# Engine orders from a list scheduler, bulk filter loads and DMA transposes in a one-core spectral and GLU kernel

## The chip, the core and the metric

The kernel runs on one core of a Trainium2 chip. The metric is device time in microseconds (us) of one execution. The engines are TensorE (PE; PEld are its weight loads), VectorE (DVE), ScalarE (ACT), GpSimd (POOL) and SyncE (SP), which issues most DMAs. Each engine runs its own list of instructions in order, and waits at an instruction until the semaphores that it names have been raised.

## What is computed

A layer norm of x, then two branches of the result that are added to x: a global filter (a two-dimensional real FFT, a product with complex weights, the inverse FFT) and a gated GELU feed-forward.

```python
x = A_x                                # 1 x 2048 x 512, bfloat16
xn = _layernorm(x, axis=-1)
# A: X = rfft2(xn) ; X = X * (w_r + 1j * w_i) ; y = irfft2(X)       w: 2048 x 257
# B: h = gelu(xn @ w_gate) * (xn @ w_up) ; y = h @ w_down           512 -> 1792 -> 512
return x + _A_ref(xn, A_w_r, A_w_i) + _B_ref(xn, B_w_gate, B_w_up, B_w_down)
```

## The kernel before

The 2048 rows of x are 16 "columns" c of 128 partitions (row 16p + c), kept in `x_t` and, normalised, in `xn`. Four columns are a block `sb` of 512 rows.

- **Loads.** SP and ACT issue x and the gate and up weights in slices, then the DFT tables (L179 to L191). The filter rows go to `TW`: 28 plain DMAs of 64 rows from SP (L206) and 18 indirect gathers of 128 rows from POOL (L208). `Wd_sb` is loaded whole behind them (L211).
- **`layernorm`** (L237): per column `bn_stats` and `bn_aggr` on DVE, the reciprocal root by ACT's Sqrt and a DVE reciprocal for the first four columns, by twelve small DVE steps (`rsqrt`, L221) for each later block, then `tensor_scalar` into `xn`.
- **`transposes`** (L254): eight PE transposes of 128x128 for two columns into PSUM (`tp`), and one DVE copy into `xnT`. All 16 columns go this way.
- **`glu`** (L412): for one of 14 slices `fc` of 128 hidden units, four matmuls with `Wg_sb` into `g_ps`, four with `Wu_sb` into `u_ps`, GELU on ACT into `ge`, the product on DVE into `hT`. Block 0 goes in halves of two columns (28 units of 256 columns), blocks 1 to 3 in units of 512 columns (42 units).
- **The filter branch.** `fold` (DVE) and `pstep` (64 PE matmuls `bp` of 128 columns, ACT copies into `Bs`) make the first DFT for a block; for each of eight groups g, `dstep` (`dp`, ACT copies `ds`), `cstep` (`ep`, ACT copies `E`), `filt` (some fifteen DVE operations with `TW`, then four DMAs F to F2 issued by SP, L364) and `icstep` (`gp`, ACT copies into `Gs`). `idstep` (`yp`) makes one column of the filter's output.
- **`down`** (L434): 14 matmuls with `Wd_sb` and one with `RI` into `y_ps`, the add of x on DVE (L443), the store (L444).

The order: the GLU units stand in a list (L449 to L455), the other steps are tasks with a due time counted in GLU time (L457 to L476), and the loop at L479 emits a task ahead of the unit at which it is due. The tile framework turns this program into each engine's list and places the waits. PSUM has four buffers with tag S and two each with G and U.

Of the kernel before, what the change touches and what calls it, by code (L numbers as in the profile page):

```python
# [28 lines left out]
def _tables():  # L29
# [80 lines left out]
    idx = np.zeros((P, NG, 2), dtype=np.int32)  # L110
    for g in range(NG):
        ks = 8 * g + 4 * h + a + 128 * kb
        if g == 0:
            ks = np.where((h == 0) & (a == 0) & (kb >= 8), 64 + 128 * (kb - 8), ks)
        idx[:, g, 0] = ks
        idx[:, g, 1] = (S - ks) % S
    idx[0, 0, 1] = S // 2
    return low(np.concatenate(parts, axis=1)), cols, low(RF), low(RI), idx.reshape(P, -1)
# [3 lines left out]
def kernel(  # L122
# [44 lines left out]
    def load_consts(first, last):
        a, b = ccols[first][0], sum(ccols[last])
        nc.sync.dma_start(out=CT[:, a:b], in_=cap[:, a:b])


    def load_x(c0, n, eng=nc.sync):
        eng.dma_start(out=x_t[:, c0:c0 + n, :], in_=x_v[:, c0:c0 + n, :])

    def load_w(a, b):
        nc.sync.dma_start(out=Wg_sb[:, :, a:b], in_=wg_v[:, :, a:b])
        nc.sync.dma_start(out=Wu_sb[:, :, a:b], in_=wu_v[:, :, a:b])

    load_x(0, 1)  # L179
    load_x(1, 1, nc.scalar)  # L180
    load_consts("ident", "ident")
    load_x(2, 2, nc.scalar)
    load_w(0, 256)
    load_w(256, 640)
    load_x(4, 4)
    load_w(640, 1216)
    load_x(8, 4)
    nc.sync.dma_start(out=RF_t[:], in_=rf_d.rearrange("p (c k) -> p c k", c=NC))
    load_w(1216, 1792)
    load_x(12, 4)  # L190
    load_consts("F0", "M0")  # L191

    W = 257
    idx_t = pc.tile([P, NG, 2], I32, name="idx_t")
    nc.gpsimd.dma_start(out=idx_t[:], in_=nc.inline_tensor(idx_np, name="spec_rows").ap()
                        .rearrange("p (g s) -> p g s", s=2))
    for T, w_in in ((TR, A_w_r), (TI, A_w_i)):  # L200
        rows = w_in.rearrange("(kb g h a) k -> h g kb a k", kb=NC, h=2, a=4)
        for g in range(NG):
            for s in range(2):
                if g > 0 and s == 0:
                    for h in range(2):
                        nc.sync.dma_start(out=T[64 * h:64 * h + 64, g, 0, 0:W], in_=rows[h, g])  # L206
                else:
                    nc.gpsimd.indirect_dma_start(  # L208
                        out=T[:, g, s, 0:W], out_offset=None, in_=w_in[:, :],
                        in_offset=bass.IndirectOffsetOnAxis(ap=idx_t[:, g, s:s + 1], axis=0))  # L210
    nc.sync.dma_start(out=Wd_sb[:], in_=wd_v)  # L211
# [4 lines left out]


    eps_t = pc.tile([P, 1], F32, name="eps_t")
    nc.vector.memset(eps_t[:], EPS)

    def rsqrt(y, var, n):  # L221

        V = nc.vector
        v = pw.tile([P, n], F32, name="v")
        t = pw.tile([P, n], F32, name="t")
        V.tensor_scalar(out=v[:], in0=var, scalar1=EPS, scalar2=None, op0=ALU.add)
        vi, ti, yi = v[:].bitcast(I32), t[:].bitcast(I32), y[:].bitcast(I32)
        V.tensor_scalar(out=ti, in0=vi, scalar1=1, scalar2=None, op0=ALU.logical_shift_right)
        V.tensor_scalar(out=yi, in0=ti, scalar1=-1, scalar2=0x5F3759DF, op0=ALU.mult, op1=ALU.add)
        for _ in range(3):  # L230
            V.tensor_tensor(out=t[:], in0=y[:], in1=y[:], op=ALU.mult)
            V.scalar_tensor_tensor(out=t[:], in0=v[:], scalar=-0.5, in1=t[:],
                                   op0=ALU.mult, op1=ALU.mult)
            V.scalar_tensor_tensor(out=y[:], in0=t[:], scalar=1.5, in1=y[:],
                                   op0=ALU.add, op1=ALU.mult)
# [18 lines left out]
    def transposes(c0):  # L254
        tp = ps.tile([P, NE, 2, P], BF16, name="tp", tag="S", bufs=4)
        for e in range(NE):
            for j in range(2):
                nc.tensor.transpose(tp[:, e, j, :], xn[:, c0 + j, e * P:(e + 1) * P], ident)  # L258
        nc.vector.tensor_copy(out=xnT[c0 // 4][:, :, c0 % 4:c0 % 4 + 2, :], in_=tp[:])


    fold_out = {}

    def fold(cg):
        V = nc.vector
# [3 lines left out]
        V.tensor_tensor(out=A[:, :, 0, :], in0=lo, in1=hi, op=ALU.add)
        V.tensor_tensor(out=A[:, :, 1, :], in0=lo, in1=hi, op=ALU.subtract)  # L270
        xf = pw.tile([P, 4, 4, P], BF16, name="xf")
        V.tensor_tensor(out=xf[:, :, 0:4:3, :], in0=A[:, :, :, 0:128], in1=A[:, :, :, 255:127:-1],
                        op=ALU.add)
        V.tensor_tensor(out=xf[:, :, 2:0:-1, :], in0=A[:, :, :, 0:128], in1=A[:, :, :, 255:127:-1],
                        op=ALU.subtract)
        fold_out[cg] = xf

    def pstep(cg, q):
        xf = fold_out[cg]
        bp = ps.tile([P, 4, P], F32, name="bp", tag="S", bufs=4)  # L280
        for j in range(4):
            nc.tensor.matmul(bp[:, j], lhsT=xf[:, j, q, :], rhs=RF_t[:, 4 * cg + j, :],  # L282
                             start=True, stop=True)
        o = Bs[:, q].rearrange("p g c r a -> p (c r) g a")[:, 8 * cg:8 * cg + 8]
        evac(o, bp[:].rearrange("p c (r g a) -> p (c r) g a", r=2, a=4))

    def evac(o, i):
        nc.scalar.copy(out=o, in_=i)  # L288
# [234 lines left out]
```

## Time and profile before

| | us |
|---|---|
| median of 3 timed runs | 198.29 (198.19 to 198.55) |
| the profiled execution, first to last instruction | 215.6 |
| PE busy in it | 184.0 |
| DVE busy | 126.2 |
| ACT busy | 90.3 |
| POOL busy | 20.3 |

The profiled execution is one run of its own, taken with the profiler on, and is 17.3 us longer than the median; the page gives no other time for it than the span. Busy time of PE counts each matmul up to its modelled end, so that neighbours overlap; the pace is read from the chain, where a group of matmuls follows another without a gap. A line such as "x4" counts the instructions in a group. [...]

### The profile page before, as it was taken

What the parts mean: (1) busy time and instruction counts of PE and PEld (TensorE: products, weight loads), DVE (VectorE), ACT (ScalarE), POOL (GpSimd) and SP (SyncE); (2) the same over time, 40 slices, a digit from 0 to 9 for tenths busy, and PEclk for the clock granted to TensorE, in tenths of its full rate; (3) what the DMA queues carried; (4) which work ended last, traced back from release to release, by engine and by line L of the source; (5) the groups of instructions that cost most, each with busy time, mean ns of one, the idle gap of its engine ahead of it and who ended that gap; (6) DMA issues with size and microseconds to landing.
All of it is one profiled execution on the core that took longest, in us unless ns stands there. A gap on an engine that the chain in (4) does not pass through costs nothing.

```text
span 215.6 us, 3193 instructions
## 1 busy us (share of the span) xinstructions
PE 184.0 (85%) x1136; PEld 102.2 (47%) x1136; DVE 126.2 (59%) x316; ACT 90.3 (42%) x170; POOL 20.3 (9%) x33
## 2 busy tenths in 40 slices
PE   0581009999889999999999899999999999999993
PEld 0451006787665545455445445444454444545441
DVE  3970006999998339978578487493353544255421
ACT  2310002353618566787778768754341212121100
POOL 1777740100000000000000000000000000000000
PEclk9998555999999999999999999999999999999999
DMA  5999732760000200101202202202002222222211
GB/s 166 362 382 380 205 76 49 223 213 3 0 2 3 97 0 2 41 19 40 49 0 52 50 0 55 49 0 49 0 3 73 73 73 85 70 91 72 77 49 49
DMA packets 17503, 17.69 MB, mean 82 GB/s; under 512 B 2208, under 2 KB 16304, under 8 KB 17488
## 3 DMA queue, kind: packets, MB, share of 16 engines
q1 hardware_dynamic: 16592, 15.90, 24.1%
q0 software_dynamic: 608, 1.19, 1.9%
q10 hardware_dynamic: 288, 0.39, 0.6%
q8 instruction: 9, 0.15, 0.3%
q14 instruction: 6, 0.05, 0.1%
HBM read 13.29 MB, written 2.10 MB: 71 GB/s over the span
## 4 chain that ended last, share of the span: by engine, by line
PE 57%; DVE 17%; another core or an unknown queue 7%; issue 6%; DMA 5%; ACT 5%; SPq 2%; DVEq 0%
PE y_ps L438 22%; PE u_ps L428 12%; PE g_ps L425 12%; ACT E L310 3%; DVE stats L242 2%; SPq L364 2%; PE tp L258 2%; DVE hT_187 L432 2%; PE dp L295 2%; PE yp L393 2%; PE y_ps L440 2%; DMA x_t<-in_A_x_dram 1%; PE bp L282 1%; DVE hT_1164 L432 1%
## 5 line engine op out<-in xcount | busy, mean ns | idle before, releaser
L431 ACT ACTIVATE ge<-g_ps 128x512 bf16<-128x512 f32 (+1 forms) x70 | 35.4, 517 | 52.2 <-PE g_ps L425 26.3
L428 PEld LDWEIGHTS <-Wu_sb 128*128 128x128 bf16 x280 | 28.3, 101 | 35.2 <-issue 14.9
L425 PEld LDWEIGHTS <-Wg_sb 128*128 128x128 bf16 x280 | 28.6, 104 | 23.2 <-issue 5.2
L443 DVE TENSOR_TENSOR y_sb<-y_ps,y_sb 128x512 bf16<-128x512 f32 x16 | 11.1, 692 | 30.2 <-PE y_ps L440 30.2
L425 PE MATMUL g_ps<-xnT_70,Wg_sb 128*128 128x256 bf16 x112 | 19.4, 300 | 10.5 <-issue 10.5
L428 PE MATMUL u_ps<-xnT_70,Wu_sb 128*128 128x256 bf16 x112 | 18.5, 297 | 7.8 <-DVE hT_187 L432 7.0
L399 ACT CAST yf<-yp 128x512 bf16<-128x512 f32 x16 | 9.2, 587 | 37.3 <-PE yp L393 37.3
L432 DVE TENSOR_TENSOR hT_187<-u_ps,ge 128x256 bf16<-128x256 f32 x28 | 11.6, 419 | 19.6 <-remote 16.0
L310 ACT CAST E<-ep 64x512 bf16<-64x512 f32 x32 | 18.5, 579 | 4.0 <-PE ep L307 3.7
L425 PE MATMUL g_ps<-xnT_72,Wg_sb 128*128 128x512 bf16 x56 | 15.4, 384 | 0.0
L425 PE MATMUL g_ps<-xnT_71,Wg_sb 128*128 128x512 bf16 x56 | 15.0, 381 | 0.0
L425 PE MATMUL g_ps<-xnT_73,Wg_sb 128*128 128x512 bf16 x56 | 14.9, 380 | 0.0
L428 PE MATMUL u_ps<-xnT_72,Wu_sb 128*128 128x512 bf16 x56 | 14.9, 379 | 0.0
L428 PE MATMUL u_ps<-xnT_73,Wu_sb 128*128 128x512 bf16 x56 | 14.9, 379 | 0.0
L428 PE MATMUL u_ps<-xnT_71,Wu_sb 128*128 128x512 bf16 x56 | 14.4, 380 | 0.0
L432 DVE TENSOR_TENSOR hT_807<-u_ps,ge 128x512 bf16<-128x512 f32 x14 | 9.6, 687 | 7.0 <-PE u_ps L428 6.7
L258 PE MATMUL tp<-CT,xn 128*128 128x128 bf16 x64 | 6.5, 243 | 7.7 <-DVE xn L250 7.6
L438 PE MATMUL y_ps<-Wd_sb,hT_187 128*128 128x512 bf16 x56 | 12.7, 379 | 0.0
L438 PE MATMUL y_ps<-Wd_sb,hT_807 128*128 128x512 bf16 x56 | 12.7, 379 | 0.0
L438 PE MATMUL y_ps<-Wd_sb,hT_1164 128*128 128x512 bf16 x56 | 12.7, 379 | 0.0
L242 DVE BATCH_NORM_STATS2 stats<-x_t 128x6 f32<-128x512 bf16 x16 | 10.6, 678 | 3.4 <-DMA x_t<-in_A_x_dram 3.4
L288 ACT CAST Bs<-bp 128x512 bf16<-128x512 f32 x16 | 8.5, 598 | 6.3 <-PE bp L282 6.3
(126 smaller groups left out, 242.0 us busy)
## 6 DMA issues: line engine op xcount, KB each, us to landing
y_sb<-in_A_x_dram SPq DMA_DIRECT2D x16, 128.0 KB
out_dram<-y_sb SPq DMA_DIRECT2D x16, 128.0 KB
Wd_sb<-in_B_w_down_dram SPq DMA_DIRECT2D x1, 1792.0 KB
x_t<-in_A_x_dram SPq DMA_DIRECT2D x3, 512.0 KB
Wg_sb<-in_B_w_gate_dram SPq DMA_DIRECT2D x2, 576.0 KB
Wu_sb<-in_B_w_up_dram SPq DMA_DIRECT2D x2, 576.0 KB
RF_t<-spec_rf SPq DMA_DIRECT2D x1, 512.0 KB
RI_t<-spec_ri SPq DMA_DIRECT2D x1, 512.0 KB
```

Source lines behind the costliest of these rows:

```text
L242: nc.vector.bn_stats(out=stats[:, j, :], in_=x_t[:, c0 + j, :])
L258: nc.tensor.transpose(tp[:, e, j, :], xn[:, c0 + j, e * P:(e + 1) * P], ident)
L288: nc.scalar.copy(out=o, in_=i)
L295: nc.tensor.matmul(dp[:, q % 2, :, q // 2], lhsT=Bs[:, q, G].rearrange("p c r a -> p (c r a)"), rhs=FQ[q], start=(q == 0), stop=(q == 3), ...
L310: nc.scalar.copy(out=E[64 * h:64 * h + 64, r], in_=ep[64 * r:64 * r + 64])
L399: nc.scalar.copy(out=yf[:, c % 2], in_=yp[:])
L425: nc.tensor.matmul(gp[:], lhsT=Wg_sb[:, e, fc * P:(fc + 1) * P], rhs=rhs[:, e, :], start=(e == 0), stop=(e == NE - 1))
L428: nc.tensor.matmul(up[:], lhsT=Wu_sb[:, e, fc * P:(fc + 1) * P], rhs=rhs[:, e, :], start=(e == 0), stop=(e == NE - 1))
L431: nc.scalar.activation(out=ge[:], in_=gp[:], func=AF.Gelu_apprx_tanh)
L432: nc.vector.tensor_tensor(out=hT[sb, fc][:, o:o + w], in0=up[:], in1=ge[:], op=ALU.mult)
L438: nc.tensor.matmul(y_ps[:], lhsT=hT[sb, f][:, cl * P:(cl + 1) * P], rhs=Wd_sb[:, f, :], start=(f == 0), stop=False)
L443: nc.vector.tensor_tensor(out=y_sb[:], in0=y_ps[:], in1=y_sb[:], op=ALU.add)
```

## The change

Every operation becomes an entry of a plan (`_Plan`): engine, duration in us, what it depends on, a priority, the buffers that it takes and uses. `run` steps through time and gives each engine, whenever it is free, the entry with the lowest priority number whose inputs are there by the durations written in it. The order found is emitted as it is, under `tc.manual_schedule()`. Beside that:

- columns 0 and 1 are normalised and transposed alone, then 2 and 3; block 0's GLU runs `fc` 0 and 1 in units of one, one and two columns, `fc` 2 to 13 in units of 512 columns;
- from column 4 on, `xnT` is written by DMA transposes issued by SP, one of 128 x 512 for each column;
- the reciprocal root is two POOL operations (`tensor_scalar`, then `tensor_tensor` with `pow`) on all columns of a step;
- filter rows: four plain loads of 64 partitions x 7 rows and two gathers of 128 x 7 rows go to `Ts`, which shares its buffer with `Wd`; twelve ACT copies (`spread`) bring them to `TW`; four gathers of one row each remain; the frequency order in the tables `RF` and `RI` is changed to suit;
- `Wd` is loaded in two halves once the spreads are done;
- nine matmuls of 512 columns on a memset tile `warm` go first on PE;
- the last column's `down`, add and store go in two halves.

```diff
+class _Plan:
+    HOP = 0.1
...
+                best = None
+                for o in ops:
+                    if any(d.end is None for d in o.deps):
+                        continue
+                    at = max([d.end + d.lag + self.HOP for d in o.deps if d.eng != "PE" or o.eng != "PE"] + [0.0])
...
+                    if best is None or (o.prio, o.n) < (best.prio, best.n):
+                        best = o
...
+    def spread(k, s, g0, g1):
+        T = (TR, TI)[k]
+        src = tiles["Ts"][:, k, s].rearrange("p (g k) -> p g k", k=KC)
+        src = src[:, g0 - 1:g1 - 1] if s == 0 else src[:, 7 - g1 + 1:7 - g0 + 1][:, ::-1]
+        nc.scalar.copy(out=T[:, g0:g1, s, 0:KC], in_=src)
...
+    NWARM = 9
+    def warm_mm(i):
+        if i == 0:
+            psum("warm", [P, D])
+        nc.tensor.matmul(tiles["warm"][:], lhsT=warm[:, 0:P], rhs=warm[:], start=True, stop=True)
...
+        e = add("POOL", 0.25, lambda: nc.gpsimd.tensor_scalar(
+            out=ve[:, k], in0=mv[:, k, 1], scalar1=1.0, scalar2=EPS, op0=ALU.mult, op1=ALU.add), ag, due - 5, lag=0.1)
+        r = add("POOL", 0.3, lambda: nc.gpsimd.tensor_tensor(
+            out=rstd[:, k], in0=ve[:, k], in1=half[:, k], op=ALU.pow), (e, o_mem[1]), due - 5, lag=0.1)
...
+    def dma_transpose(c, due):
+        XT[c] = dma(P * D * 2, lambda: nc.sync.dma_start_transpose(out=xnT[c // 4][:, :, c % 4], in_=xn[:, c]),
+                    (XN[c],), due - 30, lag=1.0)
...
+    for c0, n, due in ((0, 1, -20), (1, 1, -19), (2, 2, -18)):
+        layernorm(c0, n, due)
+        for c in range(c0, c0 + n):
+            pe_transpose(c, due)
+    for b, due in ((1, 16), (2, 24), (3, 32)):
+        layernorm(4 * b, 4, due)
+        for c in range(4 * b, 4 * b + 4):
+            dma_transpose(c, due)
...
+    units = [(0, 1, 0), (0, 1, 1), (1, 1, 0), (1, 1, 1), (2, 2, 0), (2, 2, 1)]
+    units += [(0, 4, fc) for fc in range(2, NFC)]
...
+    T_FOLD, D_FOLD = 22.0, 5.0
+    T_D, D_D = 44.0, 6.5
...
+                ex.append(dma(64 * 1024, mv_, [last] + ex[:1], t, new=(f2,) if not ex else (), use=(fb, f2), lag=0.5,
+                              issue=0.1))
...
+        parts = 2 if c == NC - 1 else 1
...
+    order = plan.run()
+    with tc.manual_schedule():
+        for o in order:
+            o.fn()
```

## Rows read from the trace of the kernel before

**Rows 1.** The page, section 1: busy us, share of the span, instructions.
```profile
PE 184.0 (85%) x1136; PEld 102.2 (47%) x1136; DVE 126.2 (59%) x316; ACT 90.3 (42%) x170; POOL 20.3 (9%) x33
```

**Rows 2.** Busy time by stretch; columns in the first line.
```profile
core 0: us, PE busy (x) PEld busy (x) DVE busy (x) ACT busy (x) POOL busy (x), PEclk, DMA share, GB/s
7.15:16.13 8.98, 7.69 (x48) 5.53 (x49) 7.17 (x18) 1.84 (x3) 6.84 (x8) 1.00 1.07 378
16.13:32.64 16.51, 1.38 (x6) 0.65 (x5) 0.56 (x3) 1.15 (x3) 10.61 (x16) 0.62 0.69 218
32.64:37.12 4.48, 4.48 (x22) 3.09 (x22) 2.77 (x10) 0.77 (x2) 0.00 (x0) 0.50 0.21 49
42.00:60.00 18.00, 16.16 (x168) 13.16 (x166) 17.84 (x58) 8.57 (x21) 0.27 (x2) 1.00 0.26 88
60.00:75.00 15.00, 14.36 (x112) 8.71 (x112) 10.71 (x29) 8.12 (x16) 0.00 (x0) 1.00 0.11 37
75.00:157.00 82.00, 79.85 (x445) 40.10 (x444) 55.38 (x125) 56.56 (x101) 0.00 (x0) 1.00 0.12 27
157.00:212.10 55.10, 55.10 (x302) 26.63 (x299) 23.21 (x48) 9.17 (x16) 0.00 (x0) 1.00 0.21 68
```

**Rows 3.** Waits: who waited for whom, us in total, times, longest us.
```profile
ACT ge L431 <- remote: 18.2, 3, 6.9
DVE hT_187 L432 <- remote: 16.0, 1, 16.0
```

**Rows 4.** The chain that ended last: start us, us, what.
```profile
0.74 2.97 DMA x_t<-in_A_x_dram
...
9.85 1.01 PE g_ps L425 x4
...
43.26 0.49 PE tp L258 x8
...
44.89 0.44 PE u_ps L428 x4
...
69.01 0.45 PE bp L282 x8
...
74.86 0.44 PE dp L295 x4
...
157.52 3.02 PE y_ps L438 x14
...
212.26 0.69 DVE y_sb L443
```

**Rows 5.** Groups by line and form: count, busy us, mean ns, idle before.
```profile
L432 DVE TENSOR_TENSOR hT_187<-u_ps,ge 128x256 bf16<-128x256 f32 x28 | 11.6, 419 | 19.6 <-remote 16.0 <-PE u_ps L428 1.7 <-issue 1.2
L242 DVE BATCH_NORM_STATS2 stats<-x_t 128x6 f32<-128x512 bf16 x16 | 10.6, 678 | 3.4 <-DMA x_t<-in_A_x_dram 3.4
L288 ACT CAST ds<-dp 128x512 bf16<-128x512 f32 x16 | 9.0, 596 | 3.1 <-PE dp L295 3.1
L208 POOL DMA_INDIRECT TW<-in_A_w_r_dram,idx_t x9 | 8.8, 981 | 6.2 <-DMA idx_t<-spec_rows 3.8 <-issue 2.4
L250 DVE TENSOR_SCALAR xn<-x_t,mv,rstd 128x512 bf16<-128x512 bf16 x16 | 5.8, 423 | 0.1
L243 DVE BATCH_NORM_AGGREGATE mv<-stats 128x2 f32<-128x6 f32 x16 | 2.6, 172 | 0.0
L234 DVE SCALAR_TENSOR_TENSOR rstd<-t,rstd 128x4 f32<-128x4 f32 x9 | 1.4, 157 | 0.1
L259 DVE COPY xnT_72<-tp 128x1024 bf16<-128x1024 bf16 x2 | 1.3, 691 | 0.0
L325 POOL TENSOR_SCALAR TW<-tt 128x8 bf16<-128x8 f32 x4 | 0.9, 258 | 0.0
```

**Rows 6.** The F exchange of one group: SP's issues, and the chain's piece.
```profile
95.68 2.38 SPq L364 DMA_DIRECT2D F_1064<-F  x4
...
97.47 2.00 DMA F_1064<-F
```

More of the change, by code (lines that the diff above doesn't have):

```diff
@@ L109, in _tables @@
     h, kb, a = np.arange(P) // 64, np.arange(P) // 4 % 16, np.arange(P) % 4
[L110 to L118, printed above, removed]
+    ks = 128 * kb + 32 * h + 8 * a
@@ L158, with cc @@
     RF_t = pc.tile([P, NC, P], BF16, name="RF_t", tag="RF")
-    late = {}
     TW = pc.tile([P, 2, NG, 2, 258], BF16, name="TW", tag="TW")
     TR, TI = TW[:, 0], TW[:, 1]
-    def cc(name, shape=None):
+    idx_t = pc.tile([P, 3], I32, name="idx_t")
+    mv = pc.tile([P, NC, nc.vector.BN_AGGR_DIM], F32, name="mv")
+    ve = pc.tile([P, NC], F32, name="ve")
+    rstd = pc.tile([P, NC], F32, name="rstd")
+    half = pc.tile([P, NC], F32, name="half")
+    warm = pc.tile([P, D], BF16, name="warm")
+    tiles = {}
+    def cc(name):
         o, w = ccols[name]
         return CT[:, o:o + w]
[L167 to L211, printed above, removed]
     ident = cc("ident")
@@ L215 @@
     IQ = [cc(f"I{q}") for q in range(4)]
[L218 to L235, printed above, removed]
@@ L254, in transposes @@
[L254 to L265, printed above, removed]
+    plan = _Plan({"S": 4, "G": 2, "U": 2, "ge": 3, "A": 1, "xf": 2, "ds": 4, "E": 2, "X": 2,
+                  "Y": 2, "F": 2, "F2": 2, "y": 3})
@@ new lines, with dve, act, pe @@
+    add = plan.op
+    PSUM_LAG = 0.2
+    OVER = {"PE": 0.0, "DVE": 0.08, "ACT": 0.08, "POOL": 0.1}
+    def dve(n, fn, deps, prio, **k):
+        return add("DVE", n, fn, deps, prio, lag=0.08, **k)
+    def act(n, fn, deps, prio, **k):
+        return add("ACT", n, fn, deps, prio, lag=0.08, **k)
+    def pe(n, fn, deps, prio, **k):
+        return add("PE", n, fn, deps, prio, lag=PSUM_LAG, **k)
+    def dma(nbytes, fn, deps, prio, eng="SP", issue=0.5, **k):
+        return add(eng, issue, fn, deps, prio, nbytes=nbytes, **k)
@@ new lines, in load_ct @@
+    def load_ct(first, last, eng="SP"):
+        a, b = ccols[first][0], sum(ccols[last])
+        q = nc.sync if eng == "SP" else nc.scalar
+        return load(P * 2 * (b - a), lambda: q.dma_start(out=CT[:, a:b], in_=cap[:, a:b]), eng=eng)
+    load_x(0, 1)
+    load_x(1, 1, "ACT")
+    d_ident = load_ct("ident", "ident", "ACT")
+    load_w(0, 2, ("SP", "ACT"))
+    load_x(2, 2)
+    load_w(2, 4)
+    load_x(4, 4)
+    load_w(4, 7)
+    load_x(8, 4)
+    load_w(7, 10)
+    load_w(10, 14)
+    load_x(12, 4)
@@ new lines, with load_wd @@
+    for k in range(2):
+        for s in range(2):
+            for g0, g1 in ((1, 3), (3, 5), (5, 8)):
+                d_tw.append(act(0.2 + (g1 - g0) * 0.215, lambda k=k, s=s, g0=g0, g1=g1: spread(k, s, g0, g1),
+                                d_st[k, s], 40 + len(d_tw)))
+    def load_wd(k):
+        if "Wd" not in tiles:
+            tiles["Wd"] = pc.tile([P, NFC, D], BF16, name="Wd_sb", tag="Wd")
+        nc.sync.dma_start(out=tiles["Wd"][:, 7 * k:7 * k + 7], in_=wd_v[:, 7 * k:7 * k + 7])
@@ new lines @@
+    d_wd = [load(P * 7 * D * 2, lambda k=k: load_wd(k), d_tw[:12]) for k in range(2)]
+    for T, w_in in ((TR, A_w_r), (TI, A_w_i)):
+        for s in range(2):
+            d_tw.append(add("POOL", 1.2, lambda T=T, w_in=w_in, s=s: nc.gpsimd.indirect_dma_start(
+                out=T[:, 0, s, 0:KC], out_offset=None, in_=w_in[:, :],
+                in_offset=bass.IndirectOffsetOnAxis(ap=idx_t[:, s:s + 1], axis=0)), (g_idx, XD[12]), 20, lag=4.0))
+    o_mem = [add("POOL", 0.3, lambda: nc.gpsimd.memset(warm[:], 1.0), (), -20, lag=0.05),
+             add("POOL", 0.2, lambda: nc.gpsimd.memset(half[:], -0.5), (), -15, lag=0.05)]
@@ L269, in fold @@
[L269 to L288, printed above, removed]
@@ new lines, with dstep, mm, ev @@
+    d_fix = add("POOL", 3.0, tables_fix, d_tw, 60, lag=0.2)
+    def dstep(G, t):
+        sb, db = _Buf("S"), _Buf("ds")
+        def mm():
+            dp = psum(f"dp.{G}", [P, 2, P, 2])
+            for q in range(4):
+                nc.tensor.matmul(dp[:, q % 2, :, q // 2], lhsT=Bs[:, q, G].rearrange("p c r a -> p (c r a)"),
+                                 rhs=FQ[q], start=(q == 0), stop=(q == 3), skip_group_check=True)
+        def ev():
+            ds = work(f"ds.{G}", [P, D], "ds")
+            nc.scalar.copy(out=ds[:], in_=tiles[f"dp.{G}"][:].rearrange("p s k t -> p (s k t)"))
+        p = pe(0.34, mm, [PS_[cg, q] for cg in range(4) for q in range(4)] + [d_ct], t, new=(sb,))
+        DS_[G] = act(0.53, ev, (p,), t - 5, new=(db,), use=(sb,)), db
@@ L434, in down @@
-    def down(c):
-        sb, cl = c // 4, c % 4
-        y_ps = ps.tile([P, D], F32, name="y_ps", tag="S", bufs=4)
-        for f in range(NFC):
-            nc.tensor.matmul(y_ps[:], lhsT=hT[sb, f][:, cl * P:(cl + 1) * P], rhs=Wd_sb[:, f, :],
-                             start=(f == 0), stop=False)
-        nc.tensor.matmul(y_ps[:], lhsT=late["RI"][:, c, :], rhs=late["yt"][:, c, :], start=False, stop=True)
-        y_sb = pw.tile([P, D], BF16, name="y_sb", bufs=3)
-        nc.sync.dma_start(out=y_sb[:], in_=x_v[:, c, :])
-        nc.vector.tensor_tensor(out=y_sb[:], in0=y_ps[:], in1=y_sb[:], op=ALU.add)
-        nc.sync.dma_start(out=out_v[:, c, :], in_=y_sb[:])
@@ L477, with mv_ @@
[L477 to L492 removed]
+                def mv_(h=h, r=r):
+                    if h == 0 and r == 0:
+                        work(f"F2.{g}", [P, 2, 2, 256], "F2")
+                    nc.sync.dma_start(out=tiles[f"F2.{g}"][64 * r:64 * r + 64, h],
+                                      in_=tiles[f"F.{g}"][64 * h:64 * h + 64, r])
@@ new lines, with load_ri @@
+    for g in range(NG):
+        t = T_D + D_D * g
+        dstep(2 * g, t)
+        dstep(2 * g + 1, t)
+        cstep(g, t + 2)
+        filt(g, t + 3)
+        icstep(g, t + 8)
+    for sb in range(1, NSB):
+        for fc in range(NFC):
+            extra = [o for cg in range(4) for o in FOLD[cg]] + [XT[c] for c in range(4, NC)] if sb == 2 else ()
+            glu(4 * sb, 4, fc, extra)
+    ID_ = {}
+    T_END = now[0]
+    all_ic = [o for g in range(NG) for o in IC_[g]]
+    d_ri = []
+    def load_ri():
+        tiles["RI"] = pc.tile([P, NC, P], BF16, name="RI_t", tag="RF")
+        nc.sync.dma_start(out=tiles["RI"][:], in_=ri_d.rearrange("p (c k) -> p c k", c=NC))
```

591 lines of the change are left out of this document (418 added, 173 removed).

## Prediction

> **What bounds the kernel now.** I read the page's first lines, then busy time by stretch, then the waits, then the chain of work that ended last, then the groups of instructions. Section 1 of the page says that PE is busy for 184.0 of 215.6 us [rows 1], so the question is what PE's time is made of. The chain gives its real pace: fourteen matmuls of 512 columns in `down` take 3.02 us (0.216 each, and the GLU's of 512 have the same shape), four of 256 columns 0.44 us (0.110 each), eight transposes 0.49 us (0.061 each), eight `bp` 0.45 us (0.056 each), four `dp` 0.44 us (0.109 each) [rows 4]. Counted by the loops in the code: 336 x 0.216 = 72.5 and 224 x 0.110 = 24.6 for the GLU, 240 x 0.216 = 51.8 for `down`, 64 x 0.061 = 3.9 for the transposes, 192 x 0.056 = 10.8 for `bp`, `gp` and `yp` (taken as equal, all 128 columns), 64 x 0.109 = 7.0 for `dp`, 16 x 0.216 = 3.5 for `ep`. That is **174.1 us of work at full pace**; the other 41.5 us of the span are lost to waits and to the lower clock.
>
> Where they are lost: 7.15 us pass before PE's first transpose, since the stretches begin there [rows 2]. From 7.15 to 16.13 PE ran 48 matmuls (16 transposes and 32 of 256 columns, 4.5 us of work in 8.98), so 4.5 are lost. From 16.13 to 32.64 it ran 6 in 16.51 us [rows 2]: 15.9 lost. [...] The last matmul is followed by the add at 212.26 [rows 4] and the store: 3.4 lost to the end of the span. 8.5 are left for 37 to 212. PE stands idle for 2.48 us in 42 to 75, for 2.15 in 75 to 157 and for none in 157 to 212 [rows 2]; in that proportion the 8.5 are about **4.5 in 37 to 75 and 4.0 in 75 to 157**. In 42 to 60 DVE is busy for 17.84 of 18 us: that stretch is bound by DVE. `down` runs without a gap.
>
> **The stop from 16.13 to 32.64 I take out of the sum.** ACT and DVE waited there 18.2 and 16.0 us for a release that the trace can place on no engine [rows 3]. The median of the timed runs is 198.29, 17.3 us under this span, and the stop with the slow clock behind it is 15.9 + 2.1 = 18.0. 215.6 - 18.0 = 197.6, so the timed runs can't contain it; the 0.7 between 197.6 and the median stays as it is on both sides.
>
> **The change, part by part.** (1) *Transposes.* 48 of the 64 leave PE: 48 x 0.061 = **2.9 off the work**; they ran between GLU matmuls, on the path. 12 DMA transposes of 128 KB take their place on SP's queue, behind all bulk loads. (2) *GLU shape.* 28 units of 256 columns become 12 of 512, two of 256 and four of 128: 24.6 becomes 96 x 0.216 + 16 x 0.110 + 32 x 0.056 = 24.3, **0.3 off**. Work after: 174.1 - 3.2 = 170.9.
>
> (3) *Start.* Before, the first GLU matmul is at 9.85 behind two-column steps [rows 4]. After, the first column goes alone: its load lands at 3.71, statistics 0.68, aggregate 0.17, two small POOL operations, normalise 0.42 [rows 4, 5], four transposes and a copy of half size. POOL's `pow` is in no row: its nearest row is 0.258 for a small POOL operation, with a hop 0.35; bounded by 0.2 below and by the 0.98 of POOL's DMA issue above I take 0.7 for the pair (0.5 to 2). At half clock a 256-column matmul takes 0.25 [rows 4], so four transposes take about 0.5, and the copy 0.4. First GLU matmul at 7.0. Columns 2 and 3 need two statistics more on DVE, POOL and two copies, and come to PE at about 10.5; by then PE has done 16 transposes and four small units, 2.8 at full pace, and small units at half pace (3.6) just fill 7.0 to 10.6. So about 7.7 are lost up to 10.5, and up to 1.2 more if the clock is still low until 13. I take **8.5 (7.5 to 10)** for the 7.15 + 4.5 = 11.65 of before.
>
> (4) *The clock.* [...] After, nine matmuls on a memset tile run from about 1.3 to 5.1 us, where PE stood idle; nothing waits for them, and their cost is nothing unless they delay the first transpose at about 5.8. [...]
>
> (5) *DVE's stage.* Off DVE in the stretch that it bounds: six copies of transposes x 0.691 = 4.1; 36 Newton steps x 0.157 = 5.6 (to two POOL operations a block); 28 products x 0.419 = 11.7 become about 10.2. Sum 11.2 of DVE's 28.6 busy us in 42 to 75 [rows 2, 5]. PE's 4.5 lost there become **1.2 (0.3 to 3)**; late next is ACT, which gets 12 spread copies. Their nearest row is 0.596 for 512 elements; at 514 and 771 elements they are 8 x 0.6 + 4 x 0.9 = 8.4 us. ACT is idle for 16 of the 33 us of 42 to 75 [rows 2], which hides them; without that cover a GELU is late by up to 0.9 each.
>
> (6) *Filter rows.* 28 SP issues and 18 gathers become 4 and 8. PE does not wait for them before or after, since the first product with them comes after `ep`: nothing. They free SP's queue, where the DMA transposes go, and 10 gathers x 0.98 on POOL, so that `pow` is not queued behind these. The second half of the loads now waits for `Wd`'s buffer to come free after the spreads, 100 us ahead of `down`: nothing.
>
> (7) *Order.* From 75 to 157 PE waits for the F exchange: four issues on SP take 2.38 us and the last lands 2.00 us after its issue [rows 6], some 3.9 in all. The plan puts `icstep` behind two modelled landings in a row, so later than 3.9. But it lets the spectral groups come closer (a group to 6.5 us, PE's own 1.75 in it): ACT's eight copies x 0.596 and 2.8 GELUs make 6.4 of that. I take **3.0 (1.5 to 5)** for 4.0. (8) *End.* The last column in halves: **3.0 (2.7 to 3.4)** for 3.4.
>
> Sum: 170.9 + 8.5 + 1.2 + 3.0 + 3.0 = 186.6, and with the 0.7 **187.3**. Best ends: 170.9 + 7.5 + 0.3 + 1.5 + 2.7 + 0.7 = 183.6. Worst: 170.9 + 10 + 3 + 5 + 3.4 + 0.7 = 193.0.
>
> **Rivals.** *A, the DMA transposes make PE wait, and the kernel gets slower.* No row shows a DMA transpose. PE reaches block 1 at about 10.5 + 2 x 0.9 + 12 x 1.73 + 1.8 (`bp`) = 35; its four columns are normalised at about 17. At t us each, one after the other, they are there at 17 + 4t. Nearest rows: a plain 128 KB load took 2.97 [rows 4], a 64 KB exchange within the chip 2.00 [rows 6]; at 3 they are there at 29 and cost nothing. At t = 7 PE waits 10 us for block 1 and 1 us more for each of the blocks 2 and 3, which are 27 us of PE apart: 12, and all is given back. From there the kernel is slower: at 8 us each 14 + 5 + 5 = 24, that is 211. For it: SP issues in order, and a queue of waiting transposes holds the F exchange too. Against: twice the nearest rows.
>
> [...]
>
> *C, the change does not do what it says.* The order written down is about the one that ran, and only the transposes, shape, start and end count: 197.6 - 2.9 - 0.3 - 3.2 - 0.4 + 0.7 = 191.5. For: before, too, each engine ran a list fixed in advance. Against: DVE's removed work is off whatever the order. *D, better.* DVE's stage and the middle lose nearly nothing and the clock is up at 10.5: 182 to 183.5.
>
> **How the numbers follow.** The forecast (183.5 to 190) 0.60, B 0.17, C 0.07, D 0.06, A 0.10. Faster by over 0.2% (what a measurement here can tell) is all but A: 0.89, with 0.01 within and 0.10 slower. The range runs from D's edge to the worst ends, 183.0 to 193.5, and leaves out A, most of D and a little of B.
>
> **What would show it.** First GLU matmul near 7.0 instead of 9.85; 16 `tp` matmuls left; no stretch with DVE full while PE waits for a product; no wait of PE for `xnT` with a DMA as releaser; the F exchange no longer a releaser of `gp`; `down` without gaps at 0.216. A stop like the one at 16 us may show or not, and says nothing of timed runs. The forecast is wrong if PE waits for `xnT`, if `pow` shows at over 1 us, or if ACT has no idle time between 40 and 100 us.

## The result and the profile after

| | before | after |
|---|---|---|
| median of the timed runs, us | 198.24 (198.06 to 198.55, 4 runs) | 188.24 (188.04 to 189.37, 4 runs) |
| the profiled execution, us | 215.6 | 186.3 |

The ratio is 0.951, with an interval of 0.948 to 0.954: 10.0 us off. The profiled execution of the changed kernel is itself one of the timed runs, 188.04 us at a span of 186.3, so 1.7 us of a time lie outside its span. The median is 0.9 above the forecast of 187.3 and well inside the range. The span was forecast at 186.6 and is 186.3: of the 0.9, 1.0 is the term for what lies outside the span (0.7 for 1.7), 0.2 is that this run is the fastest of the four, and the span takes 0.3 back.

Section 1 of the page of the changed kernel (engine, busy us, share of the span, instructions; some matmul records are missing from this trace), to be read beside [rows 1]:

```profile
PE 176.2 (95%) x1014; PEld 93.5 (50%) x1032; DVE 119.2 (64%) x264; ACT 93.2 (50%) x169; POOL 16.7 (9%) x35
```

Its busy time by stretch, to be read beside [rows 2] (PEclk is the granted share of TensorE's full clock):

```profile
core 0: us, PE busy (x) PEld busy (x) DVE busy (x) ACT busy (x) POOL busy (x), PEclk, DMA share, GB/s
7.78:9.09 1.31, 1.01 (x8) 0.84 (x9) 1.31 (x5) 0.00 (x0) 0.00 (x0) 0.53 1.03 370
9.09:13.85 4.76, 3.59 (x41) 3.24 (x40) 3.39 (x13) 1.11 (x4) 0.89 (x2) 0.77 1.07 352
13.85:40.00 26.15, 25.99 (x150) 13.65 (x154) 25.01 (x59) 15.95 (x30) 11.61 (x16) 1.00 1.09 250
40.00:75.00 35.00, 34.79 (x206) 19.02 (x208) 26.66 (x56) 29.22 (x53) 1.21 (x6) 1.00 0.31 89
75.00:127.00 52.00, 51.69 (x302) 27.47 (x307) 36.85 (x81) 37.39 (x67) 0.00 (x0) 1.00 0.16 35
127.00:131.30 4.30, 3.80 (x36) 2.42 (x35) 4.19 (x12) 3.83 (x8) 0.00 (x0) 1.00 0.00 0
131.30:183.10 51.80, 51.59 (x273) 25.64 (x275) 18.85 (x38) 4.42 (x8) 0.00 (x0) 1.00 0.23 72
```

From 13.85 us to the end of the matmuls PE stands idle for about 1.4 us in all: 0.16 + 0.21 up to 75, 0.31 + 0.50 up to 131.3, 0.21 in `down`. There is no stop. What is left to lose is ahead of 13.85. PE's list there (start, us, operation, count, and in brackets the idle time before it with its releaser):

```profile
1.31 3.64 PE L409 MATMUL warm<-warm 128*128 128x512 bf16 x9 [1.31 <-POOL half L402]
7.78 1.01 PE L444 MATMUL tp<-CT,xn 128*128 128x128 bf16 x8 [2.83 <-DVE xn L434]
9.09 0.59 PE L496 MATMUL g_ps<-xnT,Wg_sb 128*128 128x128 bf16 x4 [0.30 <-DVE xnT L447]
11.89 0.90 PE L444 MATMUL tp<-CT,xn 128*128 128x128 bf16 x8
13.85 0.61 PE L496 MATMUL g_ps<-xnT,Wg_sb 128*128 128x256 bf16 x4 [1.05 <-DVE xnT L447]
```

The first GLU matmul is at 9.09, not at 7.0, and columns 2 and 3 reach it at 13.85, not at 10.5. 16 transposes and 32 matmuls of 128 columns are 2.8 us of work, so 13.85 - 2.8 = 11.05 are lost. DVE's list says why (same columns):

```profile
4.00 1.29 DVE L421 BATCH_NORM_STATS2 st<-x_t 128x6 f32<-128x512 bf16 x2 [4.00 <-DMA x_t<-in_A_x_dram]
6.71 0.69 DVE L421 BATCH_NORM_STATS2 st<-x_t 128x6 f32<-128x512 bf16 x1 [1.21 <-DMA x_t<-in_A_x_dram]
7.33 0.72 DVE L434 TENSOR_SCALAR xn<-x_t,mv,rstd 128x512 bf16<-128x512 bf16 x2
11.06 0.29 DVE L510 TENSOR_TENSOR hT<-u_ps,ge 128x128 bf16<-128x128 f32 x1 [0.56 <-PE u_ps L496]
11.27 0.40 DVE L434 TENSOR_SCALAR xn<-x_t,mv,rstd 128x512 bf16<-128x512 bf16 x1
```

POOL has the roots of columns 0 and 1 from 6.01 to 7.11, but in the fixed order the statistics of column 2 stand ahead of `xn` of column 0, and wait until 6.71 for a load. Columns 2 and 3 have their roots at 10.52, and their `xn` stands behind a product that waits until 11.06 for matmuls, at a granted clock of 0.50 from 8.00 to 11.26.

The groups of the two POOL operations by form (busy us, mean ns of one), and the DMA transposes: SP's list (start, us of issuing) and the page's line (median us from issue to landing):

```profile
L431 POOL TENSOR_TENSOR rstd<-ve,half 128x4 f32<-128x4 f32 x3 | 3.1, 1020 | 0.2
L431 POOL TENSOR_TENSOR rstd<-ve,half 128x1 f32<-128x1 f32 x2 | 1.1, 564 | 0.1
L429 POOL TENSOR_SCALAR ve<-mv 128x1 f32<-128x1 f32 x2 | 0.4, 192 | 3.5 <-DVE mv L428 3.4
```

```profile
19.63 13.73 SPq L451 DMA_TRANSPOSE xnT<-xn  x8
xnT<-xn SPq DMA_TRANSPOSE x12, 6.3
```

No wait of PE names a transpose as its releaser.

### The profile page after: what moved, and what is told of

Same layout as the page of the kernel before. It is cut to its first block, busy times and chain, and to the rows that moved or that the text cites. A ratio compares the mean times of both kernels' runs of the same rounds, so it can differ in the third digit from the quotient of the medians.

```text
span 186.3 us, 2911 instructions
## 1 busy us (share of the span) xinstructions
PE 176.2 (95%) x1014; PEld 93.5 (50%) x1032; DVE 119.2 (64%) x264; ACT 93.2 (50%) x169; POOL 16.7 (9%) x35
## 4 chain that ended last, share of the span: by engine, by line
PE 90%; DMA 3%; DVE 2%; ACT 2%; issue 1%; SPq 0%; DVEq 0%
PE g_ps L496 26%; PE u_ps L496 26%; PE dp L600 4%; DMA x_t<-in_A_x_dram 3%; PE bp L564 2%; PE gp L737 2%; PE ep L619 2%; PE yp__1693 L837 2%; PE yp__2023 L837 2%; PE yp__1880 L837 2%; PE yp__1849 L837 2%; PE yp__1804 L837 2%; PE yp__1784 L837 2%; PE yp__1744 L837 2%; PE yp__1725 L837 2%; PE yp__2049 L837 2%
## 5 line engine op out<-in xcount | busy, mean ns | idle before, releaser
L496 PE MATMUL g_ps<-xnT,Wg_sb 128*128 128x512 bf16 (+2 forms) x232 | 58.4, 370 | 1.7 <-DVE xnT L447 1.4
L496 PE MATMUL u_ps<-xnT,Wu_sb 128*128 128x512 bf16 (+2 forms) x235 | 58.3, 368 | 0.3
L510 DVE TENSOR_TENSOR hT<-u_ps,ge 128x512 bf16<-128x512 f32 (+2 forms) x60 | 39.0, 651 | 23.5 <-PE u_ps L496 21.7
L505 ACT ACTIVATE ge<-g_ps 128x512 bf16<-128x512 f32 (+2 forms) x60 | 34.2, 570 | 32.0 <-PE g_ps L496 29.2
L837 PEld LDWEIGHTS <-hT 128*128 128x128 bf16 x238 | 23.0, 98 | 23.6 <-issue 0.2
L421 DVE BATCH_NORM_STATS2 st<-x_t 128x6 f32<-128x512 bf16 x16 | 10.4, 668 | 5.2 <-DMA x_t<-in_A_x_dram 5.2
L605 ACT CAST ds<-dp 128x512 bf16<-128x512 f32 x16 | 8.6, 592 | 2.6 <-PE dp L600 2.6
L743 ACT CAST Gs<-gp 128x512 bf16<-128x512 f32 x16 | 8.7, 589 | 0.8 <-PE gp L737 0.8
L600 PE MATMUL dp<-CT,Bs 128*128 128x128 bf16 x64 | 8.3, 309 | 0.0
L660 DVE TENSOR_TENSOR m<-X,TW 128x1024 bf16<-128x1024 bf16 x8 | 5.5, 688 | 0.2
L666 DVE TENSOR_TENSOR m<-X,TW 128x1024 bf16<-128x1024 bf16 x8 | 5.5, 682 | 0.0
```

Source lines behind the costliest of these rows:

```text
L421: V.bn_stats(out=st[:], in_=x_t[:, c])
L496: nc.tensor.matmul(p[:, 0:w], lhsT=W[:, e, fc * P:(fc + 1) * P], rhs=rhs(e), start=(e == 0), stop=(e == NE - 1))
L505: nc.scalar.activation(out=e[:, 0:w], in_=tiles[f"g_ps.{key}"][:, 0:w], func=AF.Gelu_apprx_tanh)
L510: V.tensor_tensor(out=hslot(sb, fc)[:, o:o + w], in0=tiles[f"u_ps.{key}"][:, 0:w], in1=tiles[f"ge.{key}"][:, 0:w], op=ALU.mult)
L605: nc.scalar.copy(out=ds[:], in_=tiles[f"dp.{G}"][:].rearrange("p s k t -> p (s k t)"))
L743: nc.scalar.copy(out=o, in_=tiles[f"gp.{g}.{h}"][:].rearrange("p q (n a) -> p (q n) a", a=4))
```

## The experiments

On the three chips of the experiments the kernel before took 217.04, 216.94 and 216.73 us (7 to 8 runs each, 215.2 to 219.0), with spans near 215 and mean granted clocks of 0.952 to 0.968. The profiled execution shown ahead of the prediction has 215.6 and 0.958. The changed kernel took 189.78 on the second and 190.32 on the third. No trace of the kernel before was kept on these chips, but length and clock are those of the execution with the stop from 16.13 to 32.64, so the stop is taken for a part of timed runs there. The first experiments, reckoned from 198, turned from the question of 10 us to one of 27.

**DMA transposes undone (first chip).**

```diff
-            dma_transpose(c, due)
+            pe_transpose(c, due)
```

> The changed kernel (188.2 us) with all 16 columns transposed on PE again, in the plan's order. PE gets 48 x 0.061 = 2.9 us of work back and DVE 12 copies of about 0.4. If only PE's work counts (the plan's order hides DVE): 188.2 + 2.9 = 191.1. If DVE binds the stage from 14 to 40 us, where the changed kernel has it busy for 25.0 of 26.2 us: 1 to 4 us more, 192 to 195. If the DMA transposes cost nothing and gain nothing: 188.2.

192.45 us (192.02 to 192.59), ratio to before 0.887 [0.882, 0.891]; the changed kernel as it is has 0.877 [0.872, 0.881] and 0.879 [0.876, 0.882] on the other two chips. The time lies in the range that was named for a stage bound by DVE, but from 15.49 to 132 PE has no gap, though DVE is busy for 26.42 of the 26.51 us from 15.49 to 42. The traces tell apart the 2.1 to 2.7 us between the medians. Here columns 2 and 3 begin on PE at 15.49, after a stretch at a granted clock of 0.55 (8.73 to 15.49), and from there to the end of the span it is 175.3 us. In the three traces of the changed kernel they begin at 13.85, 13.92 and 14.80, and from there it is 172.5, 172.7 and 173.0. So the 12 DMA transposes are worth 2.3 to 2.9 us, the 2.9 us of PE's work that step (1) gave them; why the start is later here is not shown.

**The root of the later blocks back on DVE (first chip).** The twelve Newton steps of before for columns 4 to 15; columns 0 to 3 keep `pow`.

```diff
+        if c0 < 4:
             e = add("POOL", 0.25, ...)
             r = add("POOL", 0.3, ...)
+        else:
+            r = newton(k, n, ag, due)
```

> The changed kernel with the reciprocal root of columns 4 to 15 by twelve small DVE steps a block instead of two POOL operations: 36 x 0.157 = 5.6 us back on DVE, in the plan's order. If it was the relief of DVE that ended PE's waits in DVE's stage: 1 to 4 us slower, 189.5 to 192. If it was the order: 188.2, within 0.4.

191.66 us (191.54 to 192.05), ratio 0.884 [0.880, 0.889]: 1.3 to 1.9 more, the time that was named for relief. But none of it lies in 42 to 75, where PE is busy throughout (18.00 of 18.00 and 15.00 of 15.00). Columns 2 and 3 begin at 15.64, and from there to the end it is 174.4 us, 1.4 to 1.9 more than in the changed kernel; 1.34 of that is one wait of PE for a GELU, ahead of 20.63. What held that GELU is not shown.

**Both undone (first chip).** The edits of the last two together.

> PE transposes for all columns and the twelve DVE steps together: 2.9 us of work back on PE and 10.5 on DVE, so DVE's load of before in the plan's order. By relief: 188.2 + 2.9 + 4.5 = 195.6. By order: 188.2 + 2.9 = 191.1.

195.12 us (194.88 to 195.26), ratio 0.900 [0.896, 0.905], nearer to the 195.6 of relief than to the 191.1 of the order. The trace says otherwise. Its busy time by stretch:

```profile
15.00:45.00 30.00, 29.11 (x170) 15.23 (x171) 27.54 (x86) 17.32 (x31) 3.92 (x9) 0.94 0.53 171
45.00:60.00 15.00, 15.00 (x107) 8.27 (x105) 14.02 (x38) 8.07 (x15) 3.03 (x6) 1.00 0.39 122
60.00:75.00 15.00, 15.00 (x95) 8.68 (x93) 8.07 (x17) 13.03 (x24) 0.00 (x0) 1.00 0.10 37
75.00:132.00 57.00, 57.00 (x336) 30.30 (x335) 45.26 (x105) 43.23 (x78) 0.00 (x0) 1.00 0.16 38
```

PE has no gap from 15.89, where columns 2 and 3 begin, to 132, though DVE has its copies and Newton steps back and is busy for 14.02 of 15 us. From 15.89 to the end it is 177.2 us, 4.2 to 4.8 more than in the changed kernel: 2.9 are the transposes' work, and a granted clock of 0.94 over the 30 us of the first row is, by estimate, another 1.8. Nothing is left for DVE. So it is not the work taken off DVE that closes the gaps of [rows 2].

**The order alone (first chip).** The plan, with before's work in it: single filter rows without spreads, PE transposes, Newton steps for the later blocks, halves of two columns in block 0, one dummy matmul, an undivided end.

```diff
-    for c0, n, due in ((0, 1, -20), (1, 1, -19), (2, 2, -18)):
+    for c0, n, due in ((0, 2, -20), (2, 2, -18)):
...
-    units = [(0, 1, 0), (0, 1, 1), (1, 1, 0), (1, 1, 1), (2, 2, 0), (2, 2, 1)]
-    units += [(0, 4, fc) for fc in range(2, NFC)]
+    units = [(0, 2, fc) for fc in range(3)]
+    for fc in range(NFC):
+        units.append((2, 2, fc))
...
-        parts = 2 if c == NC - 1 else 1
+        parts = 1
```

> The work of before in the plan's order: PE transposes, DVE steps for columns 4 to 15, block 0 in units of 256 columns, single filter rows (28 plain loads, 18 gathers) with no spread copies, one dummy matmul, the last column whole. Left from the change beside the order: POOL's root for the first four columns and the load order at the start. If the order alone ends PE's waits after 16 us: 188.2 + 2.9 (transposes) + 0.3 (shape) + 0.2 (end) + 0.5 (start) = 192.1. If the removed DVE work did: 197 to 198, as before.

213.04 us (212.52 to 213.08), ratio 0.982 [0.977, 0.987], at neither of the two expectations, since it has the stop: PE stands 3.9 us ahead of 26.53 and 8.7 ahead of 36.27. The order doesn't remove it; something that was left out of this run and stood in the last one does. Behind the stop the trace answers the question of the order:

```profile
38.00:55.00 17.00, 17.00 (x152) 14.49 (x152) 15.37 (x57) 7.50 (x19) 1.22 (x6) 0.87 0.50 149
55.00:70.00 15.00, 15.00 (x116) 9.76 (x114) 14.94 (x44) 7.16 (x15) 0.00 (x0) 1.00 0.01 2
85.00:150.00 65.00, 65.00 (x383) 35.13 (x382) 50.19 (x117) 51.79 (x95) 0.00 (x0) 1.00 0.14 34
```

With the products, copies and Newton steps of before on DVE, which is busy for 14.94 of 15 us, PE has no gap. The 4.0 us that this run gains are near the 4.6 us of gaps in 42 to 157 of the kernel before.

**The changed kernel as it is (second chip).**

> The changed kernel as it is, beside the kernel before on this chip, where that took 217.0 us beside the first four experiments and 198.2 us beside the first measurement. If the stop of the kernel before belongs to a chip and the changed kernel has none: 188 to 190 here. If everything is slower on such a chip: 200 to 206, in proportion.

189.78 us (188.38 to 190.54), no stop, PE's first transpose at 8.00.

**Filter rows as before, in the plan (second chip).** 28 loads and 18 gathers of one row each, no spreads; `Wd` waits for nothing.

```diff
-                d_tw.append(act(0.2 + (g1 - g0) * 0.215, lambda k=k, s=s, g0=g0, g1=g1: spread(k, s, g0, g1),
+        for g in range(1, NG):
+            for h in range(2):
+                d_tw.append(load(64 * KC * 2, lambda k=k, g=g, h=h: load_rows(k, g, h)))
+            d_tw.append(add("POOL", 1.2, lambda k=k, g=g: gather_rows(k, g), (g_idx, XD[12]), 20, lag=4.0))
```

> The changed kernel with the filter rows as before: 28 plain loads of 64 rows of 514 bytes from SP and 18 gathers of 128 rows from POOL straight into the table, no spread copies. If no engine waits for them, as I had it: 188.2, or 0.5 less for the freed ACT. If these small transfers are what makes the stop (semaphore updates of PE that come late, as in the profile of before and in the fourth experiment): 205 to 210 on a chip where before takes 217, and 188 where it takes 198.

209.75 us (209.17 to 210.81), ratio 0.967 [0.962, 0.971]: **20.0 us more than the changed kernel**, for a part that step (6) costed at nothing. Its waits (us in total, times, longest), two stretches, and the first and last gather on POOL:

```profile
DVE hT L495 <- remote: 17.8, 1, 17.8
PE u_ps L481 <- DVE hT L495: 16.5, 1, 16.5
```

```profile
13.00:36.50 23.50, 22.17 (x129) 11.74 (x127) 20.46 (x50) 6.42 (x12) 11.17 (x13) 1.00 0.65 193
36.50:52.80 16.30, 0.00 (x0) 0.00 (x0) 0.74 (x2) 2.63 (x5) 9.03 (x10) 0.65 1.01 227
```

```profile
25.65 1.10 POOL L361 DMA_INDIRECT TW<-in_A_w_r_dram,idx_t  x1 [0.17 <-issue]
...
47.33 0.95 POOL L380 DMA_INDIRECT TW<-in_A_w_i_dram,idx_t  x1 [0.30 <-issue]
```

It is the stop of [rows 3] at another place, and it moved with the gathers. They are issued from 25.65 to 48.28 here and PE stops from 36.5 to 52.8, that is 10.9 us after the first and to 4.5 us after the last. In the trace of before the gathers are issued from 5.77 to 28.27, and the stop is from 16.13 to 32.64: 10.4 after the first, to 4.4 after the last. The single loads did not move so (SP begins them at 14.80 before and at 15.93 here). In the packet records the gathers' last packet ends at 29.6 before and at 51.0 here, and DVE goes on at 32.2 and at 52.1. ACT waits as well (13.4 us here), not DVE alone.

**Only the gathers as before (second chip).** 18 single gathers, bulk loads.

```diff
-                d_st[k, s] = [add("POOL", 1.2, lambda k=k, s=s: load_rows(k, s, 0), (g_idx, XD[12]), 20, lag=5.0)]
+                for g in range(1, NG):
+                    d_tw.append(add("POOL", 1.2, lambda k=k, g=g: nc.gpsimd.indirect_dma_start(
```

> As the changed kernel, but with the 18 single gathers of before on POOL; the plain loads stay in bulk, with their six spread copies. If the gathers make the stop: 200 to 210 where before takes 217. If the plain loads do: 188 to 190. If only both together do: 188 to 195.

206.18 us (205.45 to 206.96), ratio 0.952 [0.947, 0.957]: 16.4 more than the changed kernel. The waits with no releaser are there, in three gaps of PE, 4.1, 2.9 and 4.1 us. The first begins 10.6 us after the first gather is issued, and the last ends 3.0 us after the last; in the run of the order alone the two long gaps lie from 11.6 after the first to 2.9 after the last. The waits:

```profile
DVE hT L515 <- remote: 13.7, 2, 8.6
ACT ge L510 <- remote: 12.8, 2, 7.9
```

**Only the loads as before (second chip).** 28 single loads, gathers in blocks.

```diff
-                d_st[k, s] = [load(64 * R7 * 2, lambda k=k, s=s, h=h: load_rows(k, s, h)) for h in range(2)]
+                for g in range(1, NG):
+                    for h in range(2):
+                        d_tw.append(load(64 * KC * 2, lambda k=k, g=g, h=h: one_row(k, g, h)))
```

> As the changed kernel, but with the 28 single plain loads of before from SP; the gathers stay in blocks, with their six spread copies. If the plain loads make the stop: 200 to 210 where before takes 217. If the gathers do: 188 to 190. SP's queue of 28 waiting loads also stands ahead of the DMA transposes: if that is what costs, PE waits for xnT and no semaphore of PE comes late.

195.42 us (194.75 to 196.10), ratio 0.901 [0.896, 0.906]: 5.6 more, and no wait without a releaser. So the single loads do not make the stop, but they cost something, and step (6) had no price for that. On SP's list the loads hold its queue, and the transposes begin at 37.41 for 19.63. PE does not wait for `xnT` there: its one long wait behind the start is 3.4 us for DVE's `xf`, ahead of 44.05, with a granted clock of 0.82 from 44.05 to 52. That the late transposes lead to that wait is not shown.

```profile
28.42 8.88 SPq L369 DMA_DIRECT2D TW<-in_A_w_i_dram  x14
37.41 7.83 SPq L459 DMA_TRANSPOSE xnT<-xn  x6
```

**Bulk rows alone, in the old order (third chip).** The kernel before with bulk loads, six gathers, twelve spreads, the new frequency order and `Wd` loaded behind the spreads.

```diff
+            nc.sync.dma_start(out=Ts[64 * h:64 * h + 64, k, 0], in_=rows[0, h][:, :, W:8 * W])
+        nc.gpsimd.indirect_dma_start(
+            out=Ts[:, k, 1], out_offset=None, in_=w_in[:, :],
+            in_offset=bass.IndirectOffsetOnAxis(ap=idx_t[:, 2:3], axis=0))
...
+                tasks.append((16 + n, lambda k=k, s=s, g0=g0, g1=g1: spread(k, s, g0, g1)))
```

> The kernel before, in its own order and with all its own work, with one part of the change alone: filter rows by four bulk loads and six gathers, twelve ACT spreads, the frequency order that goes with them, and the down weights loaded after the spreads. Theory of the gathers (the stop of some 18 us stands while the 18 single gathers of POOL are in flight): no stop, 217 less 18 = 199, and up to 2 more for the spreads on ACT, 198 to 201, ratio to the kernel before 0.91 to 0.93; PE has no gap of over 4 us between 16 and 50 us. Rival theory of the order (the stop needs the bulk rows and the plan's order together, since the run with the plan's order and single rows kept it and so may this one with the old order): 213 to 217, ratio 0.98 to 1.00. If the stop is gone, what is left between this run and the 195.1 of the run with the plan's order, small blocks and the PE and DVE work of before is what the plan's order is worth: 3 to 6 us.

204.95 us (204.50 to 205.48), ratio 0.945 [0.942, 0.947], between the two expectations. The stop is gone, and no wait lacks its releaser. One gap of 4.6 us ahead of 17.91 is this version's own: the spreads stand ahead of the first GELU in ACT's list, and wait for a gather.

```profile
12.50 3.67 ACT L216 COPY TW<-Ts 128x514 bf16<-128x514 bf16 x6 [5.42 <-DMA Ts<-in_A_w_r_dram,idx_t]
17.91 1.86 PE L434 MATMUL g_ps<-xnT,Wg_sb 128*128 128x256 bf16 x8 [4.60 <-ACT ge L440]
```

Without that gap it would be near 200, by subtraction. The old order keeps its gaps from 30 on:

```profile
30.00:45.00 15.00, 13.58 (x147) 11.04 (x145) 14.84 (x48) 10.55 (x25) 2.45 (x8) 1.00 0.31 100
45.00:60.00 15.00, 14.03 (x120) 9.30 (x118) 13.00 (x37) 7.98 (x18) 0.00 (x0) 1.00 0.08 25
75.00:145.50 70.50, 68.39 (x390) 34.29 (x388) 48.07 (x109) 49.24 (x89) 0.00 (x0) 1.00 0.15 31
```

Beside the run with both undone (195.12, the same work for DVE and all 64 transposes on PE, the plan's order, small first blocks) the 9.8 us between them are this gap and some 5 us for order, start and end: 1.42 + 0.97 + 2.11 of PE's idle time in these three stretches, none there. The 2.1 us of the last stretch are eight waits for the F exchange, which the two runs of before's work in the plan's order do not have.

**The changed kernel, the mark for the next two (third chip).**

> The changed kernel as it is, as the mark that the two runs on its start are set against on the same chip: 188 to 190, no stop, PE's first transpose at 7.8 to 8.0 us, the first GLU matmul at about 9.1, columns 2 and 3 at PE at about 13.9.

190.32 us (189.61 to 190.97); first transpose at 8.05, columns 2 and 3 at 14.80.

**x first, more dummy matmuls (third chip).** The first four columns of x in four loads ahead of all weights.

```diff
+    load_x(2, 1)
+    load_x(3, 1, "ACT")
...
-    load_x(2, 2)
...
-    NWARM = 9
+    NWARM = 15
```

> The changed kernel with the first four columns of x loaded as four single columns, from SP and ACT in turn, ahead of every weight, and with 15 dummy matmuls for 9. Theory that the start's loss of 11 us is the wait for columns 2 and 3 (their load lands at 6.7) and the clock that falls back to 0.50 before the first work: columns 2 and 3 reach PE at 11 to 12 for 13.9, the granted clock is 1.0 from the first transpose on, and the time is 2 to 4 us under the changed kernel's, about 186. Rival theory that the weights' arrival or the two POOL steps in a row on each column set the start: the first GLU matmul stays at 9 or later, and the time is within 1 us of the changed kernel's.

187.57 us (186.83 to 187.72), ratio to before 0.864 [0.861, 0.867]: **2.75 us under the changed kernel on the same chip**. PE's list:

```profile
1.31 5.37 PE L410 MATMUL warm<-warm 128*128 128x512 bf16 x15 [1.31 <-POOL half L403]
6.75 0.40 PE L445 MATMUL tp<-CT,xn 128*128 128x128 bf16 x4
9.33 0.38 PE L497 MATMUL g_ps<-xnT,Wg_sb 128*128 128x128 bf16 x4
9.55 0.39 PE L497 MATMUL u_ps<-xnT,Wu_sb 128*128 128x128 bf16 x4
11.85 1.46 PE L497 MATMUL g_ps<-xnT,Wg_sb 128*128 128x256 bf16 x8
```

The first GLU matmul is no earlier (9.33; 9.36 in the mark), but four matmuls of 128 columns follow each other in 0.22 us, not in 0.43, and columns 2 and 3 are there at 11.85. The pace and the earlier columns both show, and this run does not part what each is worth.

**One dummy matmul for nine (third chip).**

```diff
-    NWARM = 9
+    NWARM = 1
```

> The changed kernel with one dummy matmul for nine. My step (4) says the dummy matmuls cost nothing and give at most 0.8 us: the time is 0 to 0.8 us above the changed kernel's. Rival theory that they gave nothing, since the granted clock was back at 0.50 from 7.85 to 11.26 us in spite of them: within 0.3 us of the changed kernel's. If they give more than that, the clock is at 0.50 for longer than up to 11.3 us and the small units and the first units of 512 columns go at half pace: 1 to 3 us more.

189.58 us (189.07 to 189.92), not above the mark: nine dummy matmuls gave nothing that this pair can tell. In the mark they take 4.02 us, 0.43 and more each, where a matmul of 512 columns in `down` takes 0.216 [rows 4]: the pace did not rise under them, though the view prints a granted clock of 1.00 from the start on, and columns 2 and 3 come at 14.80. In the trace of the result the nine take 3.64 us, and the columns come at 13.85. What they give in an execution like that one is not measured. In the mark a group of four matmuls of 128 columns follows the last after 0.43 us (10.16, 10.59, 11.02); so it does in PE's list here:

```profile
10.22 0.63 PE L496 MATMUL u_ps<-xnT,Wu_sb 128*128 128x128 bf16 x4
10.65 0.63 PE L496 MATMUL g_ps<-xnT,Wg_sb 128*128 128x128 bf16 x4
```

## Why the prediction was right, and where it was not

**The sum came out, in part by luck.** Work: the span less all of PE's idle or lost time, 186.3 - 11.05 - 1.4 - 3.0, is 170.8, and 170.9 was predicted; steps (1) and (2) hold. Step (3), the start, was put at 8.5 (7.5 to 10) and measured 11.05, beyond its worst end. Steps (5) and (7), put at 1.2 and 3.0, are 0.4, at its best end, and 0.8 (1.0 with `down`'s), under its best end. Step (8), 3.0, is 3.0. The misses of +2.6 and -2.8 cancel, and that they do is luck. All this is read from the kernel after. No trace of an execution of the kernel before at 198 us was kept, so the 197.6 from which the sum set out is a subtraction (its 2.1 us of slow clock are the 4.48 us that 22 matmuls took behind the stop, at a granted 0.50, less 22 x 0.110 [rows 2, 4]), and the 10.0 us of the result cannot be divided into the steps by a trace of before.

**Step (3)** costed each column's chain by itself and not the order of DVE's list. The pair of POOL operations was 0.75 us for one column, as taken, but two pairs stand in a row. `pow` on four columns takes 1.02 us, over the 1 us that was named as a sign against the forecast; from block 1 on nobody on PE waits for it. And the clock: the dummy matmuls ended at 4.95, PE stood until 7.78, and the granted clock was 0.53 from 7.78 to 9.09. (The step also read 0.25 us for 256 columns at half clock off a piece of the chain that runs to a modelled end; four such matmuls follow the last four after 0.85, 0.21 each, from 11.51 on, and the view prints 1.00 there and not a half [rows 2].) **Step (4)** is right that the dummy matmuls cost nothing that shows (190.32 us with nine, 189.58 with one). The gain of at most 0.8 us, 8.5 less the 7.7 of step (3), was the author's estimate, and no run shows it. In the result's trace four matmuls of 128 columns take 0.43 us from 9.47 on, at a granted clock of 0.50 up to 11.26, and 0.22 from 11.45 on, at 1.00. With 15 dummy matmuls, ended 0.1 us ahead of the first transpose, such a four took 0.22 us from 9.33 on.

**Steps (5) and (7)** were right that the gaps close, and step (5) had the wrong cause. It was to be the 11.2 us taken off DVE. With copies and Newton steps back, PE has no gap from 45 to 132, and with all but the first four columns' root as before it has none from 38.65 to 150 in the run of the order alone; the order closes them. That is also the end of rival C (the order written down is about the one that ran): the old order keeps 4.5 us of gaps in the same stretches.

**Step (6)** fails, and with it the paragraph on the stop. "Nothing" was argued from the one consumer, PE's wait for the first product. The cost was on work that reads none of these rows: with 18 gathers under way ACT and DVE go on waiting long after PE's last matmul (with the filter rows as before in the plan, that ended at 36.30, and DVE waited until 52.06). On the second chip bulk rows are worth 20.0 of 27.2 us inside the plan (gathers alone 16.4, loads alone 5.6), more than all other parts together; on the third they take 11.8 us off the old order, with a gap of 4.6 of their own. (Step (6) also wrote eight gathers for six.) "The timed runs can't contain it" was sound for the 198 us beside which it stood, and wrong as a rule: 217 is the timed median on these chips. Why the kernel before takes 198.2 beside the result and 217 on three chips is not settled, nor is what holds the releases back while gathers are in flight: no trace has a record of it, and no run here took all gathers away, or parted their number from their size and from the time that they last.

**The rivals.** A is out, and with it B: no wait of PE names a transpose. Eight were issued in 13.73 us, one every 1.72. From issue to landing these eight took a median of 7.2 us beside the bulk loads, and the last four, issued from 38.22 on, 3.2; three plain 128 KB loads issued between the two groups took a median of 3.6. The first eight take longer than the 7 us at which A has PE wait, but they overlap, so that their pace, and not that time, is what PE could feel. D's middle came true; its early clock did not (0.50 up to 11.26).

## What to carry to other kernels

An operation's cost is not only what waits for its result: here 18 single gathers in place of six cost 16.4 us, in waits of operations that read none of their data, so look at what runs beside a stall and move it or take it away, to see whether the stall follows. In an order fixed in advance, cost a chain along each engine's list: here `xn` of column 0 stood behind statistics that waited 1.21 us for a load. Read the pace of the first real matmuls behind dummy ones: here nine that ended 2.8 us early gave no measured gain (0.107 us for 128 columns at first), and with fifteen that ran up to the first real one the pace was 0.055 us.

## What the runs showed of the hardware that was not expected

- Beside 18 single gathers, issued over 22.6 us, ACT and DVE wait 13 to 18 us for releases that the trace gives to no engine (ACT 9.4 in the run of the order alone); beside six, issued from 24.14 to 31.74, never.
- In the result's trace the pace rose during nine dummy matmuls (3.64 us for the nine, the median 0.634 us long and the shortest 0.380; 4.02 us in the mark), and the granted clock was 0.50 from 8.00 to 11.26, after PE had idled for 2.8 us; matmuls of 128 columns ran at 0.107 us each until about 11.3 us.
- In the result's trace DMA transposes of 128 x 512 were issued one every 1.72 us; the eight beside the bulk loads landed after a median of 7.2 us, the four behind them after 3.2.
- In the result's trace POOL's `pow` of a tensor by a tensor took 0.56 us for one element in each partition and 1.02 us for four.
